# Attention, expert layer and feed-forward in one kernel: the token sort for the final scatter changes its place

## The chip, the cores and the metric

One core of a Trainium2 chip runs the whole kernel in one launch. The metric is device time in microseconds (us) of that core, the median of several runs. The core has engines that run side by side, each with its own queue in program order: PE multiplies matrices, DVE does vector work, ACT does activations and copies, POOL builds small tables and scatters rows, SP issues loads. An engine waits for another only at semaphores.

## The reference, cut to what matters

```
x = banded_attention(q, k, v)                 # 2 x 576 tokens, 8 heads of 64: x is 1152 x 512
logits = x @ w_gate                           # 8 experts
e[i] = argmax(logits[i]); gate[i] = softmax(logits[i])[e[i]]
pos[i] = how many earlier tokens chose e[i]   # kept only if pos[i] < capacity = 288
h = relu(x_of_expert[e] @ w1[e])              # 512 -> 1024, for each expert
y = h @ w2[e]                                 # 1024 -> 512
z[i] = gate[i] * y[e[i], pos[i]]  or 0        # back at the token's own row
h2 = z @ w_in; g = h2 * sigmoid(h2)           # 512 -> 2048
out = g @ w_out                               # 2048 -> 512
```

The kernel keeps the tokens sorted by expert from the expert layer to the very end: column c of the expert layer's result belongs to some token, and the feed-forward part works on columns. The rows of `out` are scattered to the tokens' own places by a list `oidx` of 9 x 128 indices. Building that list is "the sort" here.

## The kernel before, in words

**Stages, in order of time.** Attention and routing run to about 98 us in the profiled execution. Then come the eight experts, one after the other (slots `p_` 0 to 7 in the order 1, 0, 2, 3, ... of `PO`), each with a first product (`layer1`, lines 957 to 959, 8 row blocks `fc`) and a second product (`layer2`, lines 982 to 988, 4 blocks `dc`). From 240 us the feed-forward part runs: `up` (lines 1434 to 1436: 16 x 3 blocks) and `down` (lines 1452 to 1454), which is done for the first six token blocks in two halves: first `fc` 0 to 7 of all six, then `fc` 8 to 15 of each with its eviction and scatter (`store`), then three token blocks whole.

**Two f16 parts.** Every f32 factor is split into a high and a low f16 part, and each product is three matmuls. ACT writes the high part, DVE the low one from the difference. For weights these are lines 229 (ACT) and 233 (DVE), 128x1024 at a time; for the experts' hidden layer lines 975 (ACT) and 976 (DVE, tile `mh`), once for two `fc`; for a second product's result lines 991 (ACT) and 992 (DVE). The weights of the feed-forward part are f64 and are also put together by DVE (lines 244, 248, 252, 271).

**What sets the order.** In the experts and the feed-forward part PE, ACT, DVE and POOL take instructions in the order in which they are written (`manual_schedule`). The conversion of weights is written between the products by `bg(credit)`, a stream that hands out pieces as a credit allows. Weights come in 1 MB loads into three staging buffers `st`; SP issues a load when DVE has finished with the buffer's last user. At the program's start another scheduler places the instructions of POOL, DVE and ACT.

**The sort before.** `order()` (lines 1253 to 1315) is a generator. `next(od, None)` at line 1330 takes a step of it at every even `fc` from the second slot on, so its DVE instructions stand between the pieces of slots 1 to 4. Its steps: `wx` and `wend` (lines 1256 to 1279) count how many extra windows overfull experts need, which ends in `ints` and decides whether the body of `tc.If` at line 1353 runs; lines 1281 to 1305 compute each token's place; lines 1310 (tile `ao`) to 1315 turn places into `oidx` by ten matmuls (`pord`, line 1314), whose instructions stand on PE in the first product of slot 4.

**In the second product** of an expert PE takes the high parts of all eight hidden blocks first and then the low ones:

```
def mm2l(py, wv, n, dc, hl):
    for c in range(KF):
        nc.tensor.matmul(py, wv[:, 0, c, d0:d0 + P], hl[:, c, :n], ...)   # line 988
```

so that the low part of the last pair of hidden blocks, the last line 976 of an expert, is asked for at c = 6 of the first block.

Of the kernel before, what the change touches and what calls it, by code (L numbers as in the profile page):

```python
# [17 lines left out]
ALU = mybir.AluOpType  # L18
AX = mybir.AxisListType
# [17 lines left out]
def kernel(  # L37
# [61 lines left out]
    capf = const.tile([P, 1], F32, name="capf")  # L99
# [563 lines left out]
    def bc(ap, T):  # L663
        return ap.unsqueeze(1).to_broadcast([P, T, E])
# [15 lines left out]
    wend = const.tile([P, E, NW], F32, name="wend")  # L680
# [5 lines left out]
    ED = E - ND  # L686
    cmp_ = const.tile([P, ED, ED], F32, name="cmp_")
# [9 lines left out]
    def cols_of(ap):  # L697
        return ap.unsqueeze(2).to_broadcast([P, ED, ED])
# [554 lines left out]
    def order():  # L1253
        yield
        for e in range(ND):
            nc.vector.memset(wx[:, e:e + 1], float(WW[e]))
        for r in range(ED):
            nc.vector.tensor_scalar(out=prod[:, r], in0=sel[:, r], scalar1=float(WW[ND + r]), scalar2=None, op0=ALU.mult)
        nc.vector.tensor_reduce(out=wx[:, ND:], in_=prod.rearrange("p r e -> p e r"), axis=AX.X, op=ALU.add)
        nc.vector.tensor_tensor(out=wx, in0=kept, in1=wx, op=ALU.subtract)  # L1260
        nc.vector.tensor_tensor(out=wx[:, 0:NS], in0=wx[:, 0:NS], in1=kepta, op=ALU.subtract)
        wa = small.tile([P, 2, NS], F32, tag="wa", name="wa", bufs=1)
# [18 lines left out]
        nc.vector.tensor_scalar(out=rk, in0=pall, scalar1=capf, scalar2=None, op0=ALU.min)  # L1281
# [4 lines left out]
        for i in range(NT):  # L1286
            nc.vector.tensor_tensor(out=rk[:, i], in0=oall[:, i], in1=sx, op=ALU.mult)
        yield
        nc.vector.tensor_reduce(out=ra, in_=rk, axis=AX.X, op=ALU.add)
        nc.vector.tensor_tensor(out=ra, in0=ra, in1=posall, op=ALU.add)  # L1290
        nc.vector.tensor_tensor(out=ra, in0=ra, in1=kb, op=ALU.subtract)
        nc.vector.tensor_scalar(out=keepall, in0=posall, scalar1=capf, scalar2=None, op0=ALU.is_lt)
# [26 lines left out]
    od = order()  # L1319
# [206 lines left out]
```

## Time and profile before

| | us |
|---|---|
| runs of the kernel before (3) | 436.55, 434.53, 435.44: median 435.44 |
| the profiled execution | 434.91 |
| its span, first to last instruction | 433.0 |
| PE busy / DVE busy / ACT busy / POOL busy | 412.5 / 285.8 / 216.0 / 159.3 |
| span up to PE's last matmul | 427.4 |

Span and execution differ by 1.9 us that lie around the instructions. PE's busy time is the union of its instructions, whose ends are modelled; gaps between its instructions show as waits with a releaser behind the arrow ("<-"). A wait is put down to the semaphore that came last. Times in the timeline count from the span's start.

### The profile page before, as it was taken

The numbers are of one execution on the slowest core, as the hardware profiler recorded it, in microseconds if no ns is written. First come the engines' busy times: TensorE is split into PE (matmuls) and PEld (weight loads), VectorE is DVE, ScalarE is ACT, GpSimd is POOL, SyncE is SP. The second block draws the span as 40 slices with busy tenths as digits, with TensorE's granted clock in tenths as the row PEclk, the third lists the DMA queues.
The fourth block names the chain that finished last, engine by engine and source line by source line (L and its number), as shares of the span: only waits on it lengthen the run. The fifth ranks groups of instructions, "written<-read, shape, count | busy, mean of one in ns | idle before, by whom it ended". The sixth has DMA issues, their size and how long they took to land. (4 is left out here: it accounts for less than half of the span.)

```text
span 433.0 us, 9399 instructions
## 1 busy us (share of the span) xinstructions
PE 412.5 (95%) x3700; PEld 297.9 (69%) x3700; DVE 285.8 (66%) x657; ACT 216.0 (50%) x425; POOL 159.3 (37%) x209
## 2 busy tenths in 40 slices
PE   5899999999998999999999899999999999999994
PEld 4577777779897989989999555555555444444441
DVE  5677878778699998888886599999899400000000
ACT  2766867455686567486753465664555300111000
POOL 4589466612512020210200376676586400111000
PEclk9999999958999999999999999999999999999999
DMA  9899845025633688889877244545430000111000
GB/s 175 162 287 243 292 162 158 3 82 172 212 133 125 223 279 317 274 296 299 306 234 240 90 137 167 161 140 185 151 141 2 0 2 0 48 51 48 26 24 24
DMA packets 51152, 65.70 MB, mean 152 GB/s; under 512 B 30230, under 2 KB 30230, under 8 KB 51106
## 3 DMA queue, kind: packets, MB, share of 16 engines
q1 hardware_dynamic: 49346, 59.79, 44.0%
q0 software_dynamic: 1760, 5.29, 3.4%
q8 instruction: 30, 0.49, 0.5%
q14 instruction: 16, 0.13, 0.1%
HBM read 60.35 MB, written 4.72 MB: 150 GB/s over the span
## 5 line engine op out<-in xcount | busy, mean ns | idle before, releaser
L1445 POOL TENSOR_TENSOR g<-th,g 128x384 f16<-128x384 f32 x48 | 67.2, 1400 | 65.6 <-ACT g L1444 65.6
L233 DVE SCALAR_TENSOR_TENSOR w_w<-st,w_w 128x1024 f16<-128x1024 f32 x56 | 67.1, 1217 | 0.7 <-issue 0.7
L229 ACT ACTIVATE w_w<-st 128x1024 f16<-128x1024 f32 x56 | 57.5, 1050 | 14.0 <-DMA st<-in_moe_w_dram 13.2
L1434 PE MATMUL pha<-yth,w_wi 128*128 128x384 f16 x192 | 62.4, 325 | 1.2 <-DVEq L1353 1.2
L1435 PE MATMUL pha<-ytl,w_wi 128*128 128x384 f16 x192 | 62.5, 325 | 0.0
L1436 PE MATMUL pha<-yth,w_wi 128*128 128x384 f16 x192 | 62.3, 324 | 0.0
L1454 PE MATMUL pob<-w_wo,g 128*128 128x512 f16 x144 | 54.6, 379 | 0.0
L1453 PE MATMUL pob<-w_wo,g 128*128 128x512 f16 x144 | 54.6, 379 | 0.0
L1452 PE MATMUL pob<-w_wo,g 128*128 128x512 f16 x144 | 54.6, 379 | 0.0
L957 PE MATMUL pmh<-mx,w_w 128*128 128x192 f16 (+6 forms) x256 | 53.4, 233 | 0.0
L958 PE MATMUL pmh<-mx,w_w 128*128 128x192 f16 (+6 forms) x256 | 53.4, 233 | 0.0
L959 PE MATMUL pmh<-mx,w_w 128*128 128x192 f16 (+6 forms) x256 | 53.3, 233 | 0.0
L1458 ACT ACTIVATE ob<-pob 128x512 f32<-128x512 f32 x9 | 5.4, 597 | 80.2 <-PE pob L1454 80.2
L920 POOL DMA_INDIRECT xs<-xbuf,gperm x12 | 15.0, 1248 | 78.1 <-PE ptm L943 76.3
L1444 ACT ACTIVATE g<-th 128x384 f16<-128x384 f32 x48 | 24.9, 519 | 31.5 <-DVE th L1440 31.5
L982 PE MATMUL pmy<-mh,w_w 128*128 128x192 f16 (+6 forms) x256 | 39.0, 233 | 0.0
L983 PE MATMUL pmy<-mh,w_w 128*128 128x192 f16 (+6 forms) x256 | 38.9, 232 | 0.0
L1459 POOL DMA_INDIRECT out_dram<-ob,oidx x9 | 8.9, 991 | 77.0 <-ACT ob L1458 77.0
L1440 DVE SCALAR_TENSOR_TENSOR th<-th,pha 128x384 f32<-128x384 f32 x48 | 26.2, 545 | 8.6 <-ACT th L1439 8.6
L1434 PEld LDWEIGHTS <-w_wi 128*128 128x128 f16 x192 | 18.6, 97 | 14.0 <-ACTq L1353 1.3
L988 PE MATMUL pmy<-mh,w_w 128*128 128x192 f16 (+6 forms) x256 | 24.0, 233 | 4.0 <-DVE mh L976 4.0
L1436 PEld LDWEIGHTS <-w_wi 128*128 128x128 f16 x192 | 18.7, 97 | 12.5
(245 smaller groups left out, 946.7 us busy)
## 6 DMA issues: line engine op xcount, KB each, us to landing
st<-in_moe_w_dram SPq DMA_DIRECT2D x28, 1024.0 KB, 5.8
st<-in_moe_w_in_dram SPq DMA_DIRECT2D x8, 1024.0 KB, 5.3
st<-in_moe_w_out_dram SPq DMA_DIRECT2D x8, 1024.0 KB, 4.9
w_w<-in_moe_w_dram SPq DMA_DIRECT2D x4, 1024.0 KB, 8.2
vst<-in_v_dram SPq DMA_DIRECT2D x8, 256.0 KB, 4.7
xbuf<-x SPq DMA_DIRECT2D x8, 256.0 KB, 3.0
qkst<-in_k_dram SPq DMA_DIRECT2D x7, 256.0 KB, 4.8
qkst<-in_q_dram SPq DMA_DIRECT2D x7, 256.0 KB, 4.8
```

Source lines behind the costliest of these rows:

```text
L229: nc.scalar.activation(out=h_, in_=sj, func=AF.Copy, scale=sc)
L233: nc.vector.scalar_tensor_tensor(out=l_, in0=sj, scalar=sc, in1=h_, op0=ALU.mult, op1=ALU.subtract)
L957: nc.tensor.matmul(ph, wv[:, 0, c, f0:f0 + P], xh[:, c, :n], start=(c == 0), stop=False)
L958: nc.tensor.matmul(ph, wv[:, 0, c, f0:f0 + P], xl[:, c, :n], start=False, stop=False)
L959: nc.tensor.matmul(ph, wv[:, 1, c, f0:f0 + P], xh[:, c, :n], start=False, stop=(c == KD - 1))
L1434: nc.tensor.matmul(ph, wv[:, 0, c, f0:f0 + P], yth[:, c, c0:c0 + BW], start=(c == 0), stop=False)
L1435: nc.tensor.matmul(ph, wv[:, 0, c, f0:f0 + P], ytl[:, c, c0:c0 + BW], start=False, stop=False)
L1436: nc.tensor.matmul(ph, wv[:, 1, c, f0:f0 + P], yth[:, c, c0:c0 + BW], start=False, stop=(c == KD - 1))
L1445: nc.gpsimd.tensor_tensor(out=gl, in0=th, in1=gh, op=ALU.subtract)
L1452: nc.tensor.matmul(po, a, wv[:, 0, fc % 8], start=(fc == 0), stop=False)
L1453: nc.tensor.matmul(po, a, wv[:, 1, fc % 8], start=False, stop=False)
L1454: nc.tensor.matmul(po, bb, wv[:, 0, fc % 8], start=False, stop=(fc == KFF - 1))
```

## The change

Four edits. (1) The part of `order()` that counts the extra windows becomes `over()` and stays in slot 1; its two loops (six multiplications by a constant, fourteen comparisons) each become one `tensor_tensor` against a table. (2) The tables `wwc` and `steps` are built at the program's start: six memsets and two iotas on POOL, one cast on DVE. (3) The rest of `order()` is written in the first half of `down`: a step after each of the token blocks 2 to 5, the remainder behind all six and behind the last weights; its ten matmuls on PE stand between the two halves. Two of its loops become one instruction each; it works on copies `rk` and `poo` and no longer changes `pall` and `posall`. (4) The same `order` is also written into the body of the `tc.If`, whose extra windows need the list early.

```diff
@@ the tables, before the attention
+    wwc = const.tile([P, ED], F32, name="wwc")
+    for r in range(ED):
+        nc.gpsimd.memset(wwc[:, r:r + 1], float(WW[ND + r]))
+    stepi = ac.tile([P, NW + NA + 1], I32, name="stepi")
+    nc.gpsimd.iota(out=stepi[:, 0:NW], pattern=[[WX, NW]], base=0, channel_multiplier=0)
+    nc.gpsimd.iota(out=stepi[:, NW:], pattern=[[P, NA + 1]], base=0, channel_multiplier=0)
+    steps = const.tile([P, NW + NA + 1], F32, name="steps")
+    nc.vector.tensor_copy(steps, stepi)
+    poo = const.tile([P, NT], F32, name="poo")
...
-    def order():
+    def over():
         yield
-        for e in range(ND):
-            nc.vector.memset(wx[:, e:e + 1], float(WW[e]))
-        for r in range(ED):
-            nc.vector.tensor_scalar(out=prod[:, r], in0=sel[:, r], scalar1=float(WW[ND + r]), scalar2=None, op0=ALU.mult)
+        nc.vector.tensor_tensor(out=prod, in0=sel, in1=cols_of(wwc), op=ALU.mult)
+        nc.vector.memset(wx[:, 0:1], float(WW[0]))
+        nc.vector.memset(wx[:, 1:2], float(WW[1]))
         nc.vector.tensor_reduce(out=wx[:, ND:], in_=prod.rearrange("p r e -> p e r"), axis=AX.X, op=ALU.add)
...
+        yield
         wa = small.tile([P, 2, NS], F32, tag="wa", name="wa", bufs=1)
...
-        for e in range(NS):
-            nc.vector.scalar_tensor_tensor(out=posall[:, CUT:], in0=oall[:, CUT:, e], scalar=ca[:, e:e + 1], in1=posall[:, CUT:],
-                                           op0=ALU.mult, op1=ALU.add)
-            nc.vector.tensor_scalar(out=pall[:, CUT:, e], in0=pall[:, CUT:, e], scalar1=ca[:, e:e + 1], scalar2=None, op0=ALU.add)
-        nc.vector.tensor_reduce(out=tot, in_=kept, axis=AX.X, op=ALU.add)
-        nc.vector.tensor_tensor(out=ints[:, E:2 * E], in0=sx, in1=kept, op=ALU.add)
         yield
-        for j in range(NW):
-            nc.vector.tensor_scalar(out=wend[:, :, j], in0=wx, scalar1=float(j * WX), scalar2=None, op0=ALU.is_gt)
-        yield
+        nc.vector.tensor_tensor(out=wend, in0=wx.unsqueeze(2).to_broadcast([P, E, NW]),
+                                in1=stepw.unsqueeze(1).to_broadcast([P, E, NW]), op=ALU.is_gt)
         nc.vector.tensor_reduce(out=nwin[:, 0:E], in_=wend, axis=AX.X, op=ALU.add)
...
+    def order(po):
+        nc.vector.tensor_reduce(out=tot, in_=kept, axis=AX.X, op=ALU.add)
+        nc.vector.tensor_copy(rk, pall)
+        nc.vector.tensor_copy(poo, posall)
...
-        for i in range(NT):
-            nc.vector.tensor_tensor(out=rk[:, i], in0=oall[:, i], in1=sx, op=ALU.mult)
+        nc.vector.tensor_tensor(out=rk, in0=oall, in1=bc(sx, NT), op=ALU.mult)
...
-        for a in range(NA + 1):
-            nc.vector.tensor_scalar(out=ge[:, :, a], in0=ra, scalar1=float(a * P), scalar2=None, op0=ALU.is_ge)
+        nc.vector.tensor_tensor(out=ge, in0=ra.unsqueeze(2).to_broadcast([P, NT, NA + 1]),
+                                in1=stepp.unsqueeze(1).to_broadcast([P, NT, NA + 1]), op=ALU.is_ge)
...
     bg(TB)
-    od = order()
+    od = over()
     for p_, e in enumerate(PO):
...
     with tc.If(n_more > 0, preferred_fallthrough_block=False):
+        for _ in order(ps_t.tile([P, 2, W], F32, tag="t", name="pord")[:, 0]):
+            pass
         nc.sync.dma_start(out=idbuf.rearrange("(t p) o -> p (t o)", p=P), in_=oidx)
...
     pos_ = [ps_a.tile([P, DM], F32, tag="a", name="pob") for t in range(TA)]
+    od = order(ps_a.tile([P, DM], F32, tag="a", name="pord"))
     for t in range(TA):
         down(pos_[t], t, 0, KFF // 2)
         bg(4 * RU)
+        if t >= 2:
+            next(od)
     bg_until(len(wunits))
+    for _ in od:
+        pass
     for t in range(TA):
         down(pos_[t], t, KFF // 2, KFF)
         store(pos_[t], t)
```

How the instructions move, at three places. First DVE in the first product of slot 1 (`mh` is the low half of a pair of hidden blocks, `w_w` a piece of weights, the rest belongs to the sort). Before, from the middle of the step behind the first `mh` to the fourth `mh`:

```order
L1268 SCALAR_TENSOR_TENSOR posall<-oall,ca,posall 128x5
L1270 TENSOR_SCALAR pall<-pall,ca 128x5
L1271 TENSOR_REDUCE tot<-kept 128x1
L1272 TENSOR_TENSOR ints<-sx,kept 128x8
L976 SCALAR_TENSOR_TENSOR mh<-pmh,mh 128x2x100
L233 SCALAR_TENSOR_TENSOR w_w_2_2506<-st_2206,w_w_2_2506 128x1024
L1275 TENSOR_SCALAR wend<-wx 128x8 x14
L976 SCALAR_TENSOR_TENSOR mh<-pmh,mh 128x2x100
L1277 TENSOR_REDUCE nwin<-wend 128x8
L1278 TENSOR_REDUCE nwin<-nwin 128x1
L1279 CAST ints<-nwin 128x9
L976 SCALAR_TENSOR_TENSOR mh<-pmh,mh 128x2x100
```

And now, from the second `mh` to the fourth:

```order
L985 SCALAR_TENSOR_TENSOR mh<-pmh,mh 128x2x100
L233 SCALAR_TENSOR_TENSOR w_w_2_2518<-st_2218,w_w_2_2518 128x1024
L1273 TENSOR_SCALAR wa<-kepta 128x1
L1274 TENSOR_SCALAR wa<-kept 128x1
L1275 TENSOR_TENSOR wa<-wa 128x1
L1276 TENSOR_TENSOR wx<-wx,wa 128x1
L985 SCALAR_TENSOR_TENSOR mh<-pmh,mh 128x2x100
L1279 TENSOR_TENSOR wend<-wx,steps 128x112
L1281 TENSOR_REDUCE nwin<-wend 128x8
L1282 TENSOR_REDUCE nwin<-nwin 128x1
L1283 CAST ints<-nwin 128x9
L985 SCALAR_TENSOR_TENSOR mh<-pmh,mh 128x2x100
```

The four instructions on `wa` moved from ahead of the second `mh` behind it, the four on `posall` to `ints` left, and fourteen comparisons became one, which now stands behind the third `mh`. In slots 2 to 4 all of the sort's rows are gone from DVE; the rows of `mh`, `w_w`, `mx` and `ytl` follow each other as before.

Second POOL at the program's start; `toki` and `posi` are integer tables, `vh` and `vl` tiles of the values, and behind the memsets of `vh` and `vl` (four pairs in both) stands the bias mask of line 407. Before:

```order
L421 IOTA iota8i 128x8
L430 IOTA toki 128x1 x10
L454 IOTA posi 128x256
L501 MEMSET vh_313 128x8
L502 MEMSET vl_314 128x8
```

Now:

```order
L430 IOTA toki 128x1 x10
L454 IOTA posi 128x256
L688 MEMSET wwc 128x1 x6
L690 IOTA stepi 128x14
L691 IOTA stepi 128x10
L501 MEMSET vh_325 128x8
L502 MEMSET vl_326 128x8
```

Eight instructions stand ahead of the bias mask that did not; on DVE the cast of `steps` stands between `tokv` (line 452) and the first `qt` (line 494).

Third DVE at the end of its queue, where `th` is the activation of an `up` block and `w_wo` the last weights. Before:

```order
L1440 SCALAR_TENSOR_TENSOR th<-th,pha 128x384
L252 SCALAR_TENSOR_TENSOR f_5707<-st_5326,f_5707 128x1024
L1440 SCALAR_TENSOR_TENSOR th<-th,pha 128x384
L271 SCALAR_TENSOR_TENSOR w_wo_5585<-f_5707,w_wo_5585 128x1024
L1440 SCALAR_TENSOR_TENSOR th<-th,pha 128x384 x2
L1521 UNCONDITIONAL_BRANCH
```

Now:

```order
L271 SCALAR_TENSOR_TENSOR w_wo_5564<-f_5686,w_wo_5564 128x1024
L1453 SCALAR_TENSOR_TENSOR th<-th,pha 128x384 x2
L1288 TENSOR_REDUCE tot<-kept 128x1
L1289 COPY rk<-pall 128x80
L1290 COPY poo<-posall 128x10
L1292 SCALAR_TENSOR_TENSOR poo<-oall,ca,posall 128x5
L1294 TENSOR_SCALAR rk<-pall,ca 128x5
L1295 TENSOR_SCALAR rk<-rk,capf 128x80
L1296 TENSOR_REDUCE kb<-rk 128x10
L1297 TENSOR_TENSOR kb<-tokf,kb 128x10
L1298 TENSOR_SCALAR kb<-kb,tot 128x10
L1300 TENSOR_TENSOR rk<-oall,sx 128x80
```

All of the sort, 32 instructions in all, stands behind the last `th` and the last weights.

## Rows read from the trace of the kernel before

**Rows 1.** PE's waits, whole span: us in total, times, longest us.
```profile
PE pmy L988 <- DVE mh L976: 4.0, 5, 1.6
```

**Rows 2.** The same waits at PE's weight load (PEld).
```profile
PEld L988 <- issue: 4.7, 5, 1.7
...
PEld L1314 <- DVE ao L1310: 1.2, 1, 1.2
```

**Rows 3.** PE's timeline, 138 to 187 us: start, us, instruction, count, [idle before <-releaser].
```profile
139.03 0.25 PE L988 MATMUL pmy<-mh,w_w 128*128 128x100 f16 x2 [1.55 <-DVE mh L976]
139.88 0.25 PE L988 MATMUL pmy<-mh,w_w 128*128 128x100 f16 x2 [0.60 <-DVE mh L976]
...
156.76 0.34 PE L988 MATMUL pmy<-mh,w_w 128*128 128x212 f16 x2 [0.90 <-DVE mh L976]
...
175.74 0.32 PE L988 MATMUL pmy<-mh,w_w 128*128 128x192 f16 x2 [0.57 <-DVE mh L976]
...
185.95 0.18 PE L1314 MATMUL pord<-ta,ao 128*128 128x9 f16 x1 [1.06 <-DVE ao L1310]
```

**Rows 4.** DVE's timeline in the first product of slot 1.
```profile
134.17 0.17 DVE L1258 TENSOR_SCALAR prod<-sel 128x6 f32<-128x6 f32 x1
...
136.18 0.36 DVE L976 SCALAR_TENSOR_TENSOR mh<-pmh,mh 128x200 f16<-128x200 f32 x1
...
137.59 1.13 DVE L1275 TENSOR_SCALAR wend<-wx 128x8 f32<-128x8 f32 x14
...
138.91 0.25 DVE L1277 TENSOR_REDUCE nwin<-wend 128x8 f32<-128x112 f32 x1
...
139.47 0.36 DVE L976 SCALAR_TENSOR_TENSOR mh<-pmh,mh 128x200 f16<-128x200 f32 x1
```

**Rows 5.** DVE's timeline in slots 2 and 3.
```profile
149.09 0.85 DVE L1287 TENSOR_TENSOR rk<-oall,sx 128x8 f32<-128x8 f16 x10
...
156.12 0.59 DVE L976 SCALAR_TENSOR_TENSOR mh<-pmh,mh 128x424 f16<-128x424 f32 x1
...
169.31 0.57 DVE L1310 TENSOR_SCALAR ao<-posf,ro 128x128 f16<-128x128 f16 x3
...
175.14 0.55 DVE L976 SCALAR_TENSOR_TENSOR mh<-pmh,mh 128x384 f16<-128x384 f32 x1
```

**Rows 6.** ACT's timeline in slots 2 and 3.
```profile
152.99 0.51 ACT L975 ACTIVATE mh<-pmh 128x424 f16<-128x424 f32 x1
...
183.70 1.06 ACT L229 ACTIVATE w_w<-st 128x1024 f16<-128x1024 f32 x1 [3.24 <-DMA st<-in_moe_w_dram]
```

**Rows 7.** Windows: length, busy us (x instructions) of PE, PEld, DVE, ACT, POOL; PEclk, DMA share, GB/s.
```profile
143.00:186.00 43.00, 40.47 (x454) 38.59 (x452) 38.75 (x85) 27.86 (x39) 4.95 (x4) 1.00 0.82 290
...
190.00:200.00 10.00, 10.00 (x125) 9.35 (x123) 8.29 (x12) 6.87 (x11) 2.67 (x2) 1.00 0.90 317
```

**Rows 8.** POOL's timeline at the start.
```profile
3.27 0.90 POOL L430 IOTA toki<- 128x1 int32 x10
4.02 0.36 POOL L454 IOTA posi<- 128x256 int32 x1
4.33 0.16 POOL L501 MEMSET vh<- 128x8 f16 x1
...
4.63 1.21 POOL L407 TENSOR_SCALAR_AFFINE_SELECT bias<-biasP 128x1024 bf16<-128x1024 bf16 x1
```

**Rows 9.** PE's timeline at the start.
```profile
5.89 0.59 PE L524 MATMUL sp<-bias,identb 128*128 128x256 bf16 x2 [1.15 <-POOL bias L407]
```

**Rows 10.** DVE's timeline at the start.
```profile
6.01 0.41 DVE L494 TENSOR_SCALAR qt<-ptf 128x256 f32<-128x256 f32 x1
```

**Rows 11.** DVE's timeline at the end of its queue.
```profile
341.35 0.55 DVE L1440 SCALAR_TENSOR_TENSOR th<-th,pha 128x384 f32<-128x384 f32 x1 [0.97 <-ACT th L1439]
```

**Rows 12.** PE's timeline where the second half of `down` begins.
```profile
365.07 0.38 PE L1452 MATMUL pob<-w_wo,g 128*128 128x512 f16 x1
```

**Rows 13.** The page, part 2: granted TensorE clock in 40 slices.
```profile
PEclk9999999958999999999999999999999999999999
```

More of the change, by code (lines that the diff above doesn't have):

```diff
@@ L686 @@
     ED = E - ND
+    wwc = const.tile([P, ED], F32, name="wwc")
[6 more added lines that the diff above has]
+    nc.vector.tensor_copy(steps, stepi)
+    stepw, stepp = steps[:, 0:NW], steps[:, NW:]
+    poo = const.tile([P, NT], F32, name="poo")
     cmp_ = const.tile([P, ED, ED], F32, name="cmp_")
@@ L1266, in order @@
         nc.vector.tensor_tensor(out=wx[:, 0:NS], in0=wx[:, 0:NS], in1=wa[:, 0], op=ALU.max)
-        for e in range(NS):
-            nc.vector.scalar_tensor_tensor(out=posall[:, CUT:], in0=oall[:, CUT:, e], scalar=ca[:, e:e + 1], in1=posall[:, CUT:],
-                                           op0=ALU.mult, op1=ALU.add)
-            nc.vector.tensor_scalar(out=pall[:, CUT:, e], in0=pall[:, CUT:, e], scalar1=ca[:, e:e + 1], scalar2=None, op0=ALU.add)
-        nc.vector.tensor_reduce(out=tot, in_=kept, axis=AX.X, op=ALU.add)
-        nc.vector.tensor_tensor(out=ints[:, E:2 * E], in0=sx, in1=kept, op=ALU.add)
         yield
-        for j in range(NW):
-            nc.vector.tensor_scalar(out=wend[:, :, j], in0=wx, scalar1=float(j * WX), scalar2=None, op0=ALU.is_gt)
-        yield
+        wend = small.tile([P, E, NW], F32, tag="ge", name="wend", bufs=1)
+        nc.vector.tensor_tensor(out=wend, in0=wx.unsqueeze(2).to_broadcast([P, E, NW]),
+                                in1=stepw.unsqueeze(1).to_broadcast([P, E, NW]), op=ALU.is_gt)
         nc.vector.tensor_reduce(out=nwin[:, 0:E], in_=wend, axis=AX.X, op=ALU.add)
@@ L1280, in order @@
         yield
-        nc.vector.tensor_scalar(out=rk, in0=pall, scalar1=capf, scalar2=None, op0=ALU.min)
+    def order(po):
+        nc.vector.tensor_reduce(out=tot, in_=kept, axis=AX.X, op=ALU.add)
+        nc.vector.tensor_copy(rk, pall)
+        nc.vector.tensor_copy(poo, posall)
+        for e in range(NS):
+            nc.vector.scalar_tensor_tensor(out=poo[:, CUT:], in0=oall[:, CUT:, e], scalar=ca[:, e:e + 1], in1=posall[:, CUT:],
+                                           op0=ALU.mult, op1=ALU.add)
+            nc.vector.tensor_scalar(out=rk[:, CUT:, e], in0=pall[:, CUT:, e], scalar1=ca[:, e:e + 1], scalar2=None, op0=ALU.add)
+        nc.vector.tensor_scalar(out=rk, in0=rk, scalar1=capf, scalar2=None, op0=ALU.min)
         nc.vector.tensor_reduce(out=kb, in_=rk, axis=AX.X, op=ALU.add)
@@ L1285, in order @@
         yield
[L1286 to L1288 removed]
+        nc.vector.tensor_tensor(out=rk, in0=oall, in1=bc(sx, NT), op=ALU.mult)
         nc.vector.tensor_reduce(out=ra, in_=rk, axis=AX.X, op=ALU.add)
[L1290 removed]
+        nc.vector.tensor_tensor(out=ra, in0=ra, in1=poo, op=ALU.add)
         nc.vector.tensor_tensor(out=ra, in0=ra, in1=kb, op=ALU.subtract)
[L1292 removed]
+        nc.vector.tensor_scalar(out=keepall, in0=poo, scalar1=capf, scalar2=None, op0=ALU.is_lt)
         nc.vector.tensor_tensor(out=ra, in0=ra, in1=keepall, op=ALU.mult)
@@ L1305, in order @@
         nc.vector.tensor_tensor(out=ta, in0=ge[:, :, 0:NA], in1=tokv.to_broadcast([P, NT, NA]), op=ALU.mult)
+        yield
         ao = small.tile([P, NT, P], F16, tag="ao", name="ao", bufs=1)
         for i in range(NT):
-            if i % 3 == 0:
+            nc.vector.tensor_scalar(out=ao[:, i], in0=posf[:, 0:P], scalar1=ro[:, i:i + 1], scalar2=None, op0=ALU.is_equal)
+            if i % 3 == 2:
                 yield
-            nc.vector.tensor_scalar(out=ao[:, i], in0=posf[:, 0:P], scalar1=ro[:, i:i + 1], scalar2=None, op0=ALU.is_equal)
-        yield
-        po = ps_t.tile([P, 2, W], F32, tag="t", name="pord")
         for i in range(NT):
-            nc.tensor.matmul(po[:, 0, 0:NA], ao[:, i], ta[:, i], start=(i == 0), stop=(i == NT - 1))
-        nc.vector.tensor_copy(oidx, po[:, 0, 0:NA])
+            nc.tensor.matmul(po[:, 0:NA], ao[:, i], ta[:, i], start=(i == 0), stop=(i == NT - 1))
+        nc.vector.tensor_copy(oidx, po[:, 0:NA])
     AD = (ENG.Activation, ENG.DVE)
     bg(TB)
-    od = order()
+    od = over()
     for p_, e in enumerate(PO):
@@ L1353 @@
     with tc.If(n_more > 0, preferred_fallthrough_block=False):
+        for _ in order(ps_t.tile([P, 2, W], F32, tag="t", name="pord")[:, 0]):
+            pass
         nc.sync.dma_start(out=idbuf.rearrange("(t p) o -> p (t o)", p=P), in_=oidx)
+        nc.vector.tensor_tensor(out=ints[:, E:2 * E], in0=sx, in1=kept, op=ALU.add)
         wbuf = dram.tile([P, 2], I32, name="wbuf")
```

2 lines of the change are left out of this document (removed).

## The prediction

> **What bounds the kernel now.** I read the page's table first: PE is busy for 412.5 of 433.0 us, so only what shortens PE's queue, or the gaps in it, shortens the kernel. The waits of PE come next. Five of them, 4.0 us together, are PE at line 988 waiting for DVE's `mh` [rows 1]; seen at the weight load, which cannot be blurred by the modelled end of the matmul before, the same five come to 4.7 us, 0.14 us more for each, and the wait of `pord` for `ao` to 1.2 us [rows 2]. The timeline of PE then says where: two waits in slot 1 (1.55 and 0.60), one in slot 2 (0.90), one in slot 3 (0.57), and `pord` in slot 4 (1.06) [rows 3]; the fifth of line 988, 0.4 us, lies in slot 7, where no sort stands. DVE's timeline shows why: in slot 1 the sort's instructions fill the queue between the second, third and fourth `mh` [rows 4], and in slots 2 and 3 they go on in front of the fourth `mh` [rows 5]. So DVE is late by the sort, PE asks for the fourth `mh` at c = 6, and the delay is PE's. In `up` and `down` PE has no such wait. What PE loses to the sort is 2.15 + 0.28 in slot 1, 0.90 + 0.14 = 1.04 in slot 2, 0.57 + 0.14 = 0.71 in slot 3 and 1.2 in slot 4.
>
> **Slot 1, part by part.** Before, 18 sort instructions stand between 134.17 and the second `mh` at 136.18: 2.01 us [rows 4], 0.11 each. Six stay there; three of them depend on the one before, so I take 0.8 us rather than 0.67, and the second `mh` starts at 134.97. From it to `wend` lie an `mh` and a weight piece, 137.59 - 136.18 = 1.41 us, which stay: 136.38. The four `wa` instructions that now follow take 0.5 (four at 0.11 to 0.2), so the third `mh` starts at 136.88, where it stood in front of 138.91 before. Then 0.28 for itself, one comparison of 112 elements in place of fourteen (its neighbour, the reduction over the same 112, took 0.25), and the three that follow, 139.47 - 138.91 = 0.56. The fourth `mh` starts at 137.97 instead of 139.47, 1.50 us earlier. PE went on 0.41 us behind its start (139.88 [rows 3]), so now at 138.38; without any wait it would be there at about 137.5, so some 0.8 us of waiting stays. Gain: 1.50 us.
>
> **Slots 2 and 3.** In slot 2, 30 instructions go: two loops of ten, one of which took 0.85 [rows 5], and ten single ones of about 0.2, in all about 3.5 us. PE now comes 1.50 earlier and wants no wait, so the fourth `mh` has to move by 1.50 + 1.04 = 2.54 from 156.12. DVE has 1.50 + 3.5 in hand. What is late next is ACT: its fourth high half started at 152.99 and took 0.51 [rows 6], so even unmoved it would let `mh` start at 153.50, and 153.58 is wanted. Gain 1.04. In slot 3 four singles and nine `ao` go, three of which took 0.57 [rows 5], together about 2.3 us; the `mh` at 175.14 has to move by 2.54 + 0.71 = 3.25 and DVE has 2.5 carried over and 2.3 of its own. Gain 0.71.
>
> **Slot 4.** The ten `pord` matmuls go, with the 1.2 us that PE stood there. The matmuls themselves cost the same in `down`, so only the wait counts. PE's lead is then 1.50 + 1.04 + 0.71 + 1.2 = 4.45 us. Slots 5 to 7 had no wait but the 0.4 in slot 7, which I leave as it is, and `up` and `down` run on PE alone, so the lead lasts to the end.
>
> **The sort in its new place.** On DVE it stands behind the last `th`, which started at 341.35 [rows 11]: 22 single instructions at about 0.2 and ten `ao` at 0.19 make 6 to 7 us, done by about 349 of the old clock. PE asks for it where the second half of `down` begins, 365.07 [rows 12]. Both move by the same lead, so 16 us of cover stand behind the price of nothing. Behind `pord` on PE stand all second halves, and behind `oidx` the first scatter; were the cover gone, each us of delay would cost one.
>
> **The start.** Eight instructions come ahead of the bias mask on POOL. Eight memsets there took the 0.30 us from 4.33 to 4.63, and ten iotas 0.90 [rows 8]. Six memsets at 0.04 and two iotas at 0.09 make 0.4 us; by whole durations, 0.16 and 0.36, they make 1.7 us. POOL is the releaser of PE's first product, which waited 1.15 us for that mask [rows 9], so this is on the path. DVE's cast of `steps` comes ahead of the first `qt`, at 6.01 [rows 10], which PE needs next: 0.1 to 0.4 more. From below the price is nothing, if a load holds that stretch anyway, though PE's wait names POOL and not a load. I take 0.5, since the rows that stand in the same queue back to back give the step; the ends are 0 and 2.1.
> The Trainium skill (GPSIMD Engine Reference, 3.1 Elementwise — side-by-side cycle accounting) speaks against this: it puts the dispatch of one DVE instruction at about 156 ns and says that POOL has two software hops where DVE has one. At no less than that the eight would take 1.25 us and the sum would end 0.85 higher, by an estimate from that page; the rows of memsets 0.04 apart do not bear it out.
>
> **Not counted.** The sort in the body of the `tc.If` is skipped as the rest of that body is. The lost writes to `ints` in `over` are one instruction of slot 1, counted above.
>
> **The sum.** 4.45 - 0.5 = 3.95 us less: the profiled execution of 434.91 becomes 430.96. That execution lies 0.53 below the median of the three, 435.44, so I forecast 431.5. With the start at 2.1 it would be 433.1, with the start at nothing 431.0.
>
> **Rival: the loads of weights hold the pace.** From slot 3 on ACT waits for weights, 3.24 us at 183.70 [rows 6], and stands with that wait in front of its own `yth` and high halves. From 143 to 186 us the loads move 290 GB/s [rows 7]; to bring the same bytes in 43 - 4.45 = 38.55 us they would need 323, and the best ten-us row of that part has 317. Against it: SP issues a load when DVE has freed a buffer, and DVE frees them earlier by what the sort took, and a rate that DVE's buffers held down is no ceiling. If the loads do not follow, the gains of slots 3 and 4 come back as waits, and 1.50 + 1.04 - 0.5 = 2.04 remain: 433.4.
> The Trainium skill (HBM Reference, Specifications (TRN2)) gives about 358 GB/s for one core; by that 323 would fit and this rival would fall. No run here shows more than 317 in that part.
>
> **Rival: a dear start.** The eight instructions cost their whole durations, and the cast its 0.4: 433.1, as above. For it: nothing but the missing rows. Against it: the steps of [rows 8].
>
> **Rival, slower: the low clock spreads.** The page shows the granted clock at half in one slice and at 0.8 in the next, around 87 to 101 us [rows 13], while PE runs many small matmuls at the end of attention and in the routing. At 1.2 GHz instead of 2.4 each us costs PE up to half a us. PE reaches this stretch 0.5 us later than before with the same work; if the clock came back only after twice the time, 14 us more at half would cost up to 7, and the time would be 438.5. It decides from 12 us more, where 6.1 are lost and the forecast has become a loss of 0.5%. Against it: nothing ahead of that stretch changes but its start, and the change takes gaps away behind it, where the clock was full in spite of them.
>
> **Rival: it does nothing.** The fourth `mh` waits for ACT and not for DVE, so the waits stay and only the start is paid: 435.9. ACT's row of 152.99 lies 3.1 us ahead of the `mh` that follows it, so this has little for it.
>
> **How the numbers follow.** Forecast 0.65, own range 430.3 to 432.8 (start from 0 to 1.7 and half a us of difference between executions); loads 0.19; dear start 0.06; low clock 0.06; nothing 0.04. The range that leaves out no more than 0.2 goes from 430.0, with all of slot 1's wait gone too, to 434.6, which takes in the loads and the dear start. About 0.5% (2.2 us, the limit 433.3) is what a measurement of this kernel tells from no change. Faster: the forecast, two thirds of the dear start and a third of the loads' rival, which lies at the limit, 0.65 + 0.04 + 0.05, and taking 0.03 off for an unseen cost 0.71. Slower: the low clock and a little for what I do not see, 0.07. The rest, 0.22, is no change.
>
> **What would show it.** In the profile after: PE's waits at line 988's successor down from 4.7 to about 1.3 at the weight load (0.8 in slot 1, 0.5 in slot 7), none of them in slots 2 and 3; no wait of `pord`; the second product of slot 1 with its fourth `mh` 1.5 us closer behind the first; POOL's bias mask 0.4 us later and PE's first product with it; the sort on DVE ended more than 10 us ahead of `pord`. The forecast is wrong if ACT's wait for weights in slots 3 and 4 grows by as much as PE's waits fall, if waits on `mh` turn up in slots 2 to 6, if PE's first product moves by over a us, or if the clock's low stretch is longer.

## The result, and the profile after

The changed kernel takes 430.55 us (median of 6 runs, 429.80 to 431.91) against 435.50 for the kernel before (6 runs, 434.48 to 437.11). The ratio of the runs is 0.9885, 95% interval 0.9859 to 0.9912, so 3.8 to 6.1 us less. The forecast was 431.5, 3.95 us less. The profiled execution took 429.99, its span 427.9; before these were 434.91 and 433.0.

First PE's waits in the profile after. Line 997 is what line 988 was, line 985 what line 976 was, line 1324 the matmuls of `pord`.

```profile
PE pmy L997 <- DVE mh L985: 1.2, 2, 0.8
PE sp L524 <- POOL bias L407: 1.2, 1, 1.2
```

The same at the weight load, where the wait is named "issue" because the matmul behind it holds the semaphore:

```profile
PEld L997 <- issue: 1.5, 2, 0.9
```

Against [rows 1, 2]: five waits on `mh` have become two, 4.7 us at the weight load have become 1.5, and `pord` is gone from the list. The wait for POOL's mask at the start is as long as it was [rows 9]. PE's timeline says which two are left (columns: start, duration, instruction, and in brackets the idle time in front of it): one in slot 1 and one in slot 7. Slots 2 and 3, where [rows 3] had 0.90 and 0.57, have none.

```profile
137.74 0.25 PE L997 MATMUL pmy<-mh,w_w 128*128 128x100 f16 x2 [0.83 <-DVE mh L985]
229.46 0.27 PE L997 MATMUL pmy<-mh,w_w 128*128 128x130 f16 x2 [0.41 <-DVE mh L985]
359.69 0.40 PE L1324 MATMUL pord<-ta,ao 128*128 128x9 f16 x10
```

DVE's timeline, first in slot 1, then the fourth `mh` of slots 2 and 3, then the sort in `down` (its first and last group) and the copy of its result:

```profile
134.26 0.36 DVE L985 SCALAR_TENSOR_TENSOR mh<-pmh,mh 128x200 f16<-128x200 f32 x1
136.17 0.36 DVE L985 SCALAR_TENSOR_TENSOR mh<-pmh,mh 128x200 f16<-128x200 f32 x1
136.45 0.27 DVE L1279 TENSOR_TENSOR wend<-wx,steps 128x112 f32<-128x112 f32 x1
137.33 0.36 DVE L985 SCALAR_TENSOR_TENSOR mh<-pmh,mh 128x200 f16<-128x200 f32 x1
...
152.15 0.59 DVE L985 SCALAR_TENSOR_TENSOR mh<-pmh,mh 128x424 f16<-128x424 f32 x1
170.44 0.55 DVE L985 SCALAR_TENSOR_TENSOR mh<-pmh,mh 128x384 f16<-128x384 f32 x1
...
336.46 0.15 DVE L1288 TENSOR_REDUCE tot<-kept 128x1 f32<-128x8 f32 x1
341.40 1.71 DVE L1320 TENSOR_SCALAR ao<-posf,ro 128x128 f16<-128x128 f16 x10
360.13 0.17 DVE L1325 CAST oidx<-pord 128x9 int32<-128x9 f32 x1 [17.01 <-PE pord L1324]
```

In slot 1 the fourth `mh` starts 3.07 us behind the second, where it was 139.47 - 136.18 = 3.29 in [rows 4], and the second starts 1.92 earlier (0.65 of that is an earlier start of the whole slot). The sort takes DVE from 336.46 to 343.1, 6.6 us, and DVE then idles 17.01 us until PE comes for `pord`. Of this, 16.6 us lie between the end of the sort and PE's first `pord` matmul at 359.69; they are the cover.

How far the stages moved, start by start, as read from the two timelines:

| first instruction of | before | after | shift |
|---|---|---|---|
| POOL's bias mask (L407) | 4.63 | 5.00 | +0.37 |
| PE's second product (L532) | 6.57 | 6.65 | +0.08 |
| slot 0, first product | 115.23 | 114.58 | -0.65 |
| slot 2, first product | 143.15 | 141.01 | -2.14 |
| slot 3, first product | 163.53 | 160.35 | -3.18 |
| slot 4, first product | 181.84 | 177.93 | -3.91 |
| slot 4, second product | 192.11 | 186.72 | -5.39 |
| feed-forward | 240.39 | 235.01 | -5.38 |
| first eviction of `down` | 370.45 | 365.32 | -5.13 |

So slot 1 gave 1.49 us, slot 2 1.04, slot 3 0.73, slot 4 1.48, of which the `pord` matmuls take 0.25 back in `down`: 4.49 together. The start cost 0.08. Another 0.73 came between PE's second product and slot 0, where the change does nothing.

### The profile page after: what moved, and what is told of

Same layout as the page of the kernel before. It is cut to its first block, busy times and chain, and to the rows that moved or that the text cites. A ratio compares the mean times of both kernels' runs of the same rounds, so it can differ in the third digit from the quotient of the medians.

```text
span 427.9 us, 9375 instructions
## 1 busy us (share of the span) xinstructions
PE 411.6 (96%) x3700; PEld 297.6 (70%) x3700; DVE 284.2 (66%) x623; ACT 215.8 (50%) x425; POOL 158.0 (37%) x217
## 5 line engine op out<-in xcount | busy, mean ns | idle before, releaser
L929 POOL DMA_INDIRECT xs<-xbuf,gperm x12 | 14.1, 1172 | 74.3 <-PE ptm L952 72.5
L991 PE MATMUL pmy<-mh,w_w 128*128 128x192 f16 (+6 forms) x256 | 39.0, 233 | 0.0
L992 PE MATMUL pmy<-mh,w_w 128*128 128x192 f16 (+6 forms) x256 | 38.9, 232 | 0.0
L1447 PEld LDWEIGHTS <-w_wi 128*128 128x128 f16 x192 | 18.6, 97 | 13.9 <-ACTq L1363 1.3
L1449 PEld LDWEIGHTS <-w_wi 128*128 128x128 f16 x192 | 18.7, 97 | 12.5
L1448 PEld LDWEIGHTS <-w_wi 128*128 128x128 f16 x192 | 18.6, 97 | 12.6
```

The source lines that it names most:

```text
L1447: nc.tensor.matmul(ph, wv[:, 0, c, f0:f0 + P], yth[:, c, c0:c0 + BW], start=(c == 0), stop=False)
L1448: nc.tensor.matmul(ph, wv[:, 0, c, f0:f0 + P], ytl[:, c, c0:c0 + BW], start=False, stop=False)
L1449: nc.tensor.matmul(ph, wv[:, 1, c, f0:f0 + P], yth[:, c, c0:c0 + BW], start=False, stop=(c == KD - 1))
```

## The experiments

Three questions were open: whether the two halves of the change do what their slots show, how much cover the sort has in `down`, and where the time beyond 4.49 - 0.08 = 4.41 comes from.

**1. The counting alone.** The kernel before with the tables and the loop-free counting; the rest of the sort stays in slots 2 to 4.

```
-        for r in range(ED):
-            nc.vector.tensor_scalar(out=prod[:, r], in0=sel[:, r], scalar1=float(WW[ND + r]), ...)
+        nc.vector.tensor_tensor(out=prod, in0=sel, in1=cols_of(wwc), op=ALU.mult)
...
-        for j in range(NW):
-            nc.vector.tensor_scalar(out=wend[:, :, j], in0=wx, scalar1=float(j * WX), ...)
+        nc.vector.tensor_tensor(out=wend, in0=wx..., in1=stepw..., op=ALU.is_gt)
```

> The kernel before with only the counting of extra windows written without loops (tables at the start, three shorter steps in slot 1); the sort stays in slots 2 to 4, with the four instructions on posall to ints now at the head of slot 2. Theory (each wait of PE on the low half is DVE's lateness by the sort, and lasts to the end): the fourth low half of slot 1 comes 1.5 us earlier, slot 2's wait grows by the 0.4 us of the four instructions, slots 3 and 4 keep theirs: about 1.0 us less than before, 434.5. Rival (the gain in slot 1 is given back at once, since slot 2 waits for DVE again): slot 2's wait at the weight load grows from 1.1 to 2.6 and the time is that of before, 435.5. On the 0.7 us that the changed kernel won ahead of slot 0, where nothing was changed: if it is the landing of the last rows of x, which varies from run to run, this kernel may show either value; if the new tables did it, this kernel has them too and shows PE at slot 0 by 0.6 earlier than before.

Measured 433.08 (12 runs) against 435.23 for before (24 runs on the same chip), ratio 0.9949 (0.9933 to 0.9966). PE's timeline and its waits at the weight load:

```profile
138.88 0.25 PE L996 MATMUL pmy<-mh,w_w 128*128 128x100 f16 x2 [0.83 <-DVE mh L984]
```
```profile
PEld L996 <- issue: 3.2, 4, 1.1
PEld L1322 <- DVE ao L1318: 1.5, 1, 1.5
```

Slot 1 gained 1.47, slots 2 and 3 kept their waits (the 0.4 that the expectation added to slot 2 did not show), and in slot 4 `pord` waited 0.3 longer. That is 1.2 us over the slots, but the runs are 2.2 us faster (1.5 to 2.9). The mechanism in slot 1 was as expected; the rest is taken up in experiments 7 and 8 and behind them.

**2. The move of the sort alone.** The changed kernel with the loops back in place and without the tables.

```
-        nc.vector.tensor_tensor(out=prod, in0=sel, in1=cols_of(wwc), op=ALU.mult)
+        for r in range(ED):
+            nc.vector.tensor_scalar(out=prod[:, r], in0=sel[:, r], scalar1=float(WW[ND + r]), ...)
```

> The changed kernel without its tables: the sort is in the second product of the feed-forward part, the counting of extra windows has its loops again. Theory: slot 1 wins only the 0.4 us of the four instructions that left, slots 2, 3 and 4 win 1.06, 0.73 and 1.2: 3.4 less than before, 432.1, with a wait of about 2.0 at the weight load in slot 1 and none in slots 2 to 4. Rival (loads of weights hold the pace behind slot 1): less than 2 us, 433.5 or more, with new waits in slots 3 and 4. On slot 0: without tables, PE at slot 0 stands where it stood before if the tables did it, and anywhere between if it is the landing of x.

Measured 432.15 (7 runs), ratio 0.9939 (0.9917 to 0.9960). PE waited in slot 1 and nowhere in slots 2 to 6:

```profile
138.63 0.25 PE L989 MATMUL pmy<-mh,w_w 128*128 128x100 f16 x2 [1.14 <-DVE mh L977]
139.47 0.31 PE L989 MATMUL pmy<-mh,w_w 128*128 128x100 f16 x2 [0.60 <-DVE ints L1275]
```

Slots 2, 3 and 4 gave 1.05, 0.73 and 1.48, as in the changed kernel. Slot 1 has 0.4 us less of waiting than before, as expected, and yet was 1.2 us longer in this execution, with a granted clock of 0.50 behind the waits. The two halves are thus separable: the waits of slot 1 belong to the counting, those of slots 2 to 4 to the move.

**3. The ten matmuls alone.** The kernel before with `pord` and the copy of `oidx` moved between the halves of `down`; DVE's part of the sort stays.

```
-        po = ps_t.tile([P, 2, W], F32, tag="t", name="pord")
-        for i in range(NT):
-            nc.tensor.matmul(po[:, 0, 0:NA], ao[:, i], ta[:, i], ...)
+        sorted_ao.extend([ao, ta])
...
     bg_until(len(wunits))
+    order_pe(pord)
```

> The kernel before with only the ten matmuls of the sort and the copy of the list moved between the halves of the second feed-forward product; all vector work of the sort stays in slots 1 to 4. Theory: slot 4 gets 1.47 us shorter, the ten matmuls cost 0.25 in their new place, the waits in slots 1 to 3 stay: 1.2 less than before, 434.3. Rival (the wait for ao hides a wait for something later in slot 4, such as the first weights or the low half): slot 4 keeps a wait on line 988 of about a us, and the time is that of before, 435.5.

Measured 433.82 (12 runs), ratio 0.9985 (0.9965 to 1.0004): not told from no change, though the profile shows slot 4 1.48 us shorter and `down` 0.26 longer. Its profiled execution lost 1.6 us in slot 1 at half the granted clock and got part of it back when the wait in slot 2 vanished. So the term of slot 4 is confirmed by the stage, not by the time.

**4. The counting later.** The changed kernel with the steps of `over` taken in slot 6 (and 7) instead of slot 1.

```
-            elif fc % 2 == 0:
+            elif p_ >= 6 and fc % 2 == 0:
                 next(od, None)
```

> The changed kernel with the counting of extra windows taken in slot 6 instead of slot 1. In the changed kernel the fourth low half of slot 6 is ready 1.9 us before PE asks, and DVE stands idle for 1.0 in that product; the counting takes 2.1. Theory: slot 1's last wait (0.9 at the weight load) goes and slot 6 gets none: 0.8 less than the changed kernel, 429.7. Rival (the counting only moves its wait along): a wait of 0.3 to 0.9 on the low half in slot 6, and the time is that of the changed kernel, 430.5.

Measured 430.03 (6 runs), ratio to before 0.9893 (0.9867 to 0.9918). No wait on `mh` is left in slots 1 or 6:

```profile
139.05 0.20 PE L991 MATMUL pmy<-mh,w_w 128*128 128x100 f16 x1 [0.50 <-issue]
...
229.36 0.27 PE L997 MATMUL pmy<-mh,w_w 128*128 128x130 f16 x2 [0.41 <-DVE mh L985]
```

But PE then stood in slot 1 for nothing that the profile shows ("issue"), and slot 2 began only 0.09 us earlier against slot 1. Neither theory foresaw this; what the stall is stays open. The time lies between the two expectations, and six runs do not tell it from the 430.55 of the changed kernel.

**5. The cover.** The changed kernel with DVE's part of the sort carried out twice, and five times, in `down`; the repeats write the same values and leave out the last of the ten `ao`.

```
         bg(4 * RU)
+        if t == 1:
+            for _ in range(4):                 # 1 for twice
+                for k, _ in enumerate(order(None)):
+                    if k == 5:
+                        break
```

> After, with the DVE part of the sort carried out twice in its new place (the second copy overwrites the first with the same values). One copy is about 6.3 us of DVE. Theory (16.6 us of cover between the end of the sort, 343.1, and the first pord matmul, 359.7): the end moves to about 349.5, nobody waits, time 430.5, ratio to before 0.989. Rival (the second product also waits for DVE's weight pieces, which now queue behind the sort, so DVE has no room there): 6 us more, 436.8.

> After, with the DVE part of the sort carried out five times in its new place. Theory (a cover of 16.6 us): four copies of 6.3 us are 25.2, the sort ends at about 368.3 and PE stands 8.6 us in front of pord: 439.2, and from there on each us of delay costs one. Rival (the weight pieces on DVE behind the copies are needed earlier than pord is): more than 10 us, above 441; rival (cover is larger than the trace shows, since the second halves could start without pord): 430.5.

Twice: 430.71 (4 runs), ratio 0.9892 (0.9866 to 0.9917). Five times: 439.18 (4 runs), ratio 1.0083 (1.0060 to 1.0107); the kernel before, run beside them, 435.00. Twice, DVE's timeline (the last group of the sort and the copy):

```profile
347.87 1.71 DVE L1320 TENSOR_SCALAR ao<-posf,ro 128x128 f16<-128x128 f16 x10
360.86 0.17 DVE L1325 CAST oidx<-pord 128x9 int32<-128x9 f32 x1 [11.27 <-PE pord L1324]
```

Five times, PE's timeline, and then PE's busy time and granted clock in stretches (PEclk is the column behind the engines, 1.00 for 2.4 GHz and 0.50 for 1.2):

```profile
365.82 1.65 PE L1324 MATMUL pord<-ta,ao 128*128 128x9 f16 x10 [4.86 <-DVE ao L1320]
```
```profile
360.00:364.00 4.00, 0.96 (x5) 0.23 (x3) 3.69 (x23) 0.00 (x0) 0.00 (x0) 1.00 0.00 0
364.00:366.00 2.00, 0.18 (x2) 0.12 (x2) 1.82 (x10) 0.00 (x0) 0.00 (x0) 0.77 0.00 0
368.00:370.00 2.00, 2.00 (x6) 0.76 (x5) 0.00 (x0) 0.00 (x0) 0.00 (x0) 0.50 0.01 4
372.00:374.00 2.00, 2.00 (x11) 0.93 (x10) 0.00 (x0) 0.00 (x0) 0.00 (x0) 1.00 0.00 0
```

One copy more shortens DVE's idle time from 17.01 to 11.27 us and costs nothing, so the cover is real. With four copies more the sort ends at about 367.2 and PE, which came at 360.96, loses 6.3 us (4.86 in front of `pord`, then ten matmuls spread over 1.65 instead of 0.40). The first eviction is 8.9 us later than with one copy more. Of the rest, 0.4 us lay ahead of `down` already, in slot 4, and 2.3 are PE at half clock behind the wait. The time was the expected one by luck: it is made of less waiting and of a clock that was not in the expectation.

**6. The price of the start.** The kernel before with the new instructions of the start alone, unused, four times over.

```
+    for _ in range(4):
+        for r in range(ED):
+            nc.gpsimd.memset(wwc[:, r:r + 1], float(WW[ND + r]))
+        nc.gpsimd.iota(out=stepi[:, 0:NW], ...)
+        nc.gpsimd.iota(out=stepi[:, NW:], ...)
+    nc.vector.tensor_copy(steps, stepi)
```

> Before, with the change's new instructions at the start alone, unused and four times over: 24 memsets and 8 iotas on POOL ahead of the bias mask, and one cast on DVE. By the steps of 0.035 and 0.09 us POOL is 1.6 us later, and the mask with it. Theory (the start of the change cost next to nothing because DVE's mask of tokens, 1.04 us beside POOL's mask, takes 0.16 when POOL's mask comes later): PE's second product loses 1.6 - 1.0 + 0.3 = 0.9 us, time 436.4. Rival (the step of the prediction, 0.5 for each copy): 2.0 us, 437.5. Rival (a load holds the start anyway): 435.5.

Measured 436.47 (10 runs), ratio 1.0035 (1.0017 to 1.0053), 1.5 us more. POOL's timeline has the mask at 6.13, 1.50 later, DVE's shows what happens beside it, and PE's what follows:

```profile
5.38 0.26 POOL L691 MEMSET wwc<- 128x1 f32 x6
6.13 1.09 POOL L407 TENSOR_SCALAR_AFFINE_SELECT bias<-biasP 128x1024 bf16<-128x1024 bf16 x1
```
```profile
4.66 0.16 DVE L434 SCALAR_TENSOR_TENSOR tokn<-tokf,valid 128x10 f32<-128x10 f32 x1
6.21 1.04 DVE L695 CAST steps<-stepi 128x24 f32<-128x24 int32 x1 [1.17 <-POOL stepi L693]
7.17 0.41 DVE L494 TENSOR_SCALAR qt<-ptf 128x256 f32<-128x256 f32 x1
```
```profile
7.79 1.23 PE L532 MATMUL sp<-kt,qt 64*128 64x128 f32 x8
```

One copy takes POOL 0.37 us, as in the changed kernel. PE's second product is 1.22 later, not 0.9: the cast of `steps` itself ran into POOL's mask and took 1.04 us, as `tokn` does before. The price of the start is thus set by which DVE instruction lies beside the mask. The time is not that price alone: the profiled execution, 434.72, reaches slot 0 only 0.39 later than before (115.62) and lies below the median of before, so that the expected 436.4 was met in part by luck.

**7. A longer wait in slot 1.** The changed kernel with one multiplication of the counting done twenty times.

```
-        nc.vector.tensor_tensor(out=prod, in0=sel, in1=cols_of(wwc), op=ALU.mult)
+        for _ in range(20):
+            nc.vector.tensor_tensor(out=prod, in0=sel, in1=cols_of(wwc), op=ALU.mult)
```

> After, with one 128x36 multiplication of the counting carried out twenty times in slot 1, ahead of the second mh: some 2.6 us more of DVE, so that PE waits about 3.4 us in all there (0.8 in after, 2.15 in before). Nothing else is changed. Theory (a wait of about 2 us and more in slot 1 is followed by a stretch of a few us at half the granted clock, as in the profiles of the sort alone and of the matmuls alone): slot 1 loses 2.6 plus 0.6 to 1.2, time 433.8 to 434.4, and the profile shows a stretch at 0.5 behind the wait. Rival (the clock there falls by chance and has nothing to do with the wait): 2.6 more, 433.2, full clock behind it.

Measured 435.70 (10 runs), ratio to before 1.0026 (1.0010 to 1.0042); 5.0 us over the run of experiment 5 with two copies, on the same chip. PE's timeline, then the stretches behind it:

```profile
139.93 0.25 PE L997 MATMUL pmy<-mh,w_w 128*128 128x100 f16 x2 [2.30 <-DVE mh L985]
141.85 0.33 PE L997 MATMUL pmy<-mh,w_w 128*128 128x100 f16 x2 [1.67 <-DVE mh L985]
143.00 0.33 PE L997 MATMUL pmy<-mh,w_w 128*128 128x100 f16 x2 [0.83 <-DVE mh L985]
```
```profile
138.00:140.00 2.00, 0.07 (x2) 0.07 (x2) 1.78 (x12) 1.87 (x3) 1.10 (x2) 1.00 0.77 270
140.00:142.00 2.00, 0.33 (x4) 0.22 (x4) 1.91 (x7) 0.65 (x1) 0.00 (x0) 0.71 0.22 68
144.00:146.00 2.00, 2.00 (x27) 2.00 (x26) 1.65 (x3) 0.58 (x2) 0.00 (x0) 0.50 0.01 4
148.00:150.00 2.00, 2.00 (x32) 2.00 (x29) 1.31 (x3) 1.28 (x2) 0.00 (x0) 1.00 1.02 422
```

The multiplications took 4.55 us, not the 2.6 that I had expected, and PE waited 4.8 us instead of 3.4. From slot 1 to slot 2 this execution took 6.55 us more than the changed kernel: 4.0 are waiting, 2.55 are work at 1.2 GHz. The direction of the theory holds, its size did not. The profiled execution is the slowest of the ten.

**8. The kernel before, twice more.** No edit; for its profile.

> Before once more, for its profile alone. Theory (in some executions of before the granted clock falls behind the 2.15 us of waiting in slot 1, which explains the half us that the medians differ by beyond the slots): a run of about 435.5 or more shows a stretch at 0.5 that begins near 140 us and slot 2 begins 0.6 to 1.2 us later against slot 1 than in the first profile; a run of about 434.2 shows none. Rival: a run above 435.5 shows full clock there and is late elsewhere.

> Before a third time, for its profile, with the same expectation as the second: if its time is 435.5 or more, a stretch at 0.5 near 140 us; if about 434.2, none.

They took 436.01 and 434.77. In both PE waits 1.55 to 1.56 and 0.60 us in slot 1. Stretches of the first, then of the second:

```profile
138.00:140.00 2.00, 0.34 (x4) 0.22 (x4) 1.93 (x17) 2.00 (x3) 1.58 (x2) 0.92 0.60 162
140.00:142.00 2.00, 2.00 (x26) 2.00 (x26) 1.59 (x4) 0.44 (x1) 0.00 (x0) 0.50 0.42 148
142.00:144.00 2.00, 2.00 (x36) 2.00 (x35) 2.00 (x3) 1.28 (x2) 0.00 (x0) 0.73 0.22 14
```
```profile
140.00:142.00 2.00, 2.00 (x49) 2.00 (x48) 1.59 (x4) 1.11 (x3) 0.00 (x0) 1.00 0.41 135
```

The same wait in the same code is followed by half the clock in one execution and by the full clock in the other. Where it fell, slot 2 began 1.5 us later than in the profile that the prediction was made from; the wait in slot 2 swallowed 1.05 of that, slots 3 and 4 lost 0.6 more, and 1.05 us stayed to the end. That profile is one of those without.

**9. A version that aims at the last wait.** The kernel of experiment 4 with fewer weight pieces beside the first product of slot 7.

```
-    R1, R2 = [0.0033] * E, [0.008] * E
+    R1, R2 = [0.0033] * (E - 1) + [0.0020], [0.008] * E
```

> After, with the counting taken in slot 6 instead of slot 1 (as in the run on slot 6) and the share of weight pieces that runs beside slot 7's first product cut from 0.0033 to 0.0020 for each unit, so that DVE's fourth mh there is not behind a piece. Theory (the last wait of PE on mh, 0.4 to 0.5 us in slot 7, goes and nothing takes its place): 429.5. Rival (as in the run on slot 6, where the wait in slot 1 went and a stall without a releaser took its place): 430.0. Rival (the pieces not done in slot 7 hold up the first product behind it): 430.8.

Measured 429.89 (6 runs, 428.52 to 430.35), ratio to before 0.9861 (0.9832 to 0.9889). No wait on `mh` is left; the stall of experiment 4 is there again:

```profile
140.31 0.21 PE L992 MATMUL pmy<-mh,w_w 128*128 128x100 f16 x1 [0.46 <-issue]
```

From slot 7 to the feed-forward part PE gained 0.58 us, and 0.20 went in slot 4. It has the lowest median of all; from the changed kernel (430.55) these runs do not tell it apart.

## Why the prediction was right, and where it was not

**Slots 1 to 4.** Forecast 1.50, 1.04, 0.71 and 1.2, found 1.49, 1.04, 0.73 and 1.48 - 0.25 = 1.23. The reading that each wait of PE there was DVE's queue, and that ACT's margin was large enough, held; in slot 2 ACT's fourth high half ended at 151.58, 0.57 ahead of DVE's `mh`. (The rows have 19 sort instructions in front of the second `mh`, not 18; at 0.11 each this changes nothing.) In slot 2 the fourth `mh` started 3.97 us earlier than in [rows 5], of which 0.65 is the earlier slot; 2.54 were wanted. It ended at 152.74, 0.8 us before PE's seventh matmul of line 997 at 153.58. The 0.8 us that was said to stay in slot 1 is there as 0.83.

**The sort in `down`.** Forecast 6 to 7 us on DVE and 16 us of cover; found 6.6 and 16.6. Experiment 5 showed the cover. The step that failed is the aside that each us beyond it costs one: 6.3 us lost there were followed by 2.3 more at half the clock.

**The start.** This term was mis-sized: 0.5 forecast, 0.08 found. POOL's part was right (0.4 forecast, 0.37 found), and as the mask itself took 1.09 instead of 1.21, PE's first product came only 0.25 later. The estimate from the dispatch figure of the Trainium skill (GPSIMD Engine Reference, 3.1 Elementwise — side-by-side cycle accounting), 1.25 us for the eight instructions, is refuted by that 0.37. What I missed lies on DVE: [rows 10] show `qt` at 6.01, and I read this as an instruction with its place in the queue. In fact `tokn`, three instructions ahead, had been held for 1.04 us. In the profile after it takes 0.16:

```profile
4.63 0.16 DVE L434 SCALAR_TENSOR_TENSOR tokn<-tokf,valid 128x10 f32<-128x10 f32 x1
4.94 0.18 DVE L693 CAST steps<-stepi 128x24 f32<-128x24 int32 x1
5.03 0.42 DVE L494 TENSOR_SCALAR qt<-ptf 128x256 f32<-128x256 f32 x1
```

because POOL's mask began only at 5.00, behind the tables. So `qt` came 0.98 us earlier, and PE's second product followed the first after 0.51 us (6.14 to 6.65) instead of 0.68 (5.89 to 6.57). Of the delay of 0.25, 0.17 was paid back there.

**What was not in the sum.** In the profiled pair 0.73 us came between PE's second product and slot 0. Most of it is a wait that only the profile of before has. At 105.5 us PE of the changed kernel is 0.11 behind; then it takes up the rows of `x` that POOL has gathered (`xs`), without a wait, while before it waited for them twice (two lines of before, then one of after):

```profile
109.00 0.30 PE L943 MATMUL pt<-ident,xs 128*128 128x128 f32 x1 [0.27 <-DMA xs<-xbuf,gidx]
109.53 1.65 PE L943 MATMUL pt<-ident,xs 64*128 64x64 f32 x7 [0.22 <-DMA xs<-xbuf,gidx]
108.67 1.86 PE L952 MATMUL pt<-ident,xs 128*128 128x128 f32 x8
```

POOL's gather started at 101.77 before and at 100.43 after. It is not the change: slot 0 begins at 115.21 to 115.27 in the three profiles of before, and between 114.56 (experiment 4) and 115.86 (experiment 9) in kernels with the changed start. The run with two copies of the sort has the code of the changed kernel up to `down`, and its slot 0 begins at 115.33, without a wait for the gather. There the stretch at half clock near 90 us was longer, some 17 us instead of 13.65: from 86 to 103 us the granted clock is 0.50 throughout, in the changed kernel 0.60 on average. Experiments 3 and 7 show these 17 us too, and experiment 3 has the code of before up to there. What makes the stretch longer stays open.

In the medians, something else can fill the gap: before stands 2.15 us in slot 1, and in some executions the clock then falls to half, which left 1.05 us in the one profile of before that shows it. The changed kernel waits 0.8 there, and its profile shows the full clock. 4.41 us of stages and a part of 1.05 lie within 3.8 to 6.1.

The record has the mean granted clock of every execution, which allows a rough cut, made afterwards. Of the 54 executions of before that ran beside the experiments, 22 had 0.979 or more, with a median of 434.47; the other 32 have 435.56. Of the changed kernel two had 0.981 and 0.982 and took 429.99 and 429.80; four had 0.976 to 0.978, median 430.75. At like clock the kernels differ by 4.6 to 4.8 us, nearer to 4.41 than the 4.95 of the medians. For the counting alone the same cut gives 1.4 to 1.6 in place of 2.2, with 1.2 in its slots, for the ten matmuls alone 0.9 to 1.1, with 1.2 in slot 4, and for the move alone 2.4 to 2.5, where its slots 2 to 4 gave 3.3 and slot 1 lost 1.2 at half clock. So a part of what the medians have beyond the slots goes with the clock. How much of it falls in slot 1 stays open, since the mean does not say where the clock fell: the third profile of before has 0.976 with the full clock in slot 1 and a stretch at half clock between 50 and 60 us, and took 434.77.

**The rivals.** The loads did not hold the pace. The stretch from 143 to 186 us of [rows 7], after 141 to 182, and a later stretch:

```profile
141.00:182.00 41.00, 41.00 (x459) 39.51 (x457) 33.28 (x41) 28.10 (x40) 4.23 (x4) 1.00 0.90 306
187.00:195.00 8.00, 8.00 (x112) 8.00 (x110) 7.08 (x11) 5.82 (x8) 3.17 (x2) 1.00 1.01 357
```

306 GB/s in place of 290, and 357 over 8 us where the best row before had 317: that row was no ceiling. The trace of before had shown more in shorter windows, 406 GB/s from 146 to 148 us. ACT waits longer for weights (13.0 us from 141 to 194, before 11.1 from 143 to 200), but the waits do not reach PE. The start was not dear. The low clock did not spread in the profiled pair: the stretch near 90 us lies from 87.40 to 101.05, before from 87.27 to 100.92 [rows 13]. It can last 17 us, as said above, but does so with the code of before as well, and with two copies of the sort slot 0 then began 0.75 later than in the changed kernel, not the several us of the rival. Where the clock bears on the medians, it does so with the other sign. And the change does what it says.

## What to carry to other kernels

Read each wait of the bound engine back to the queue that filled it, and move the filler to where that engine will not ask for long; then the gain is the wait itself, slot by slot, as long as the next releaser has margin. A wait can cost more than its length where half the clock follows it, so a profile of one execution may understate what its removal is worth. Before pricing an instruction that is put in front of others, look for a neighbour whose duration is out of line with its size: it may be waiting for another engine, and the shift may free it.

## What was not expected of the hardware

**DVE instructions held for as long as one of POOL runs.** The text ahead of the prediction says that an engine waits for another only at semaphores; here DVE stands for POOL without one, and the profile shows it as busy time. A DVE instruction on 128x10 took 1.04 us from 4.81 to 5.85 beside POOL's mask (4.63 to 5.84), and 0.16 without it. In experiment 6 a cast on 128x24 took 1.04, from 6.21 to 7.25, beside the mask (6.13 to 7.22). In `down` the same happens to the sort. With two copies of it (experiment 5), the first minimum (line 1295) lies beside a POOL product that starts at 337.89 and takes 0.92, the second beside none:

```profile
337.95 0.90 DVE L1295 TENSOR_SCALAR rk<-rk,capf 128x80 f32<-128x80 f32 x1
344.36 0.26 DVE L1295 TENSOR_SCALAR rk<-rk,capf 128x80 f32<-128x80 f32 x1
```

Each of the three ends within 0.05 us of POOL's instruction. Not every instruction is held: after the change `qt`, which reads PE's result, ran from 5.03 to 5.45 beside the mask (5.00 to 6.09) and took 0.42, as before without it (0.41). The Trainium skill (SBUF — State Buffer, SBUF: two separate sides) has this: a pair of ports that the two engines share is locked for a whole instruction by whichever starts first, and the other fully blocks; on DVE's side it names instructions with two inputs in SBUF and those in a mode that uses two ports. The trace agrees with blocking, 1.04 against 0.16 us; which mode an instruction ran in no view shows.

**The clock behind a wait.** Six profiles have 1.7 to 2.2 us of waiting in slot 1, in two pieces. Behind it PE's granted clock fell to 0.50 in three (experiments 2 and 3, the second profile of before) and stayed at 1.00 in three (the first and third of before, experiment 6). It also fell behind 4.8 us in experiment 7 and behind the wait for `pord` in experiment 5. Behind 0.8 us in slot 1 it stayed at 1.00 in four profiles (after, experiment 1, both of experiment 5). What decides between the two stays open.
